# Unit scale of a scan-and-route kernel: from sums of squares ahead of the scan, in place of a largest value after it

## The chip, the cores and the metric

The kernel runs on one core of a Trainium2 chip. Its engines run side by side and meet through semaphores: TensorE (PE, with its weight loads as PEld), VectorE (DVE), ScalarE (ACT), GpSimd (POOL) and the DMA queues, of which SyncE (SP) issues most. The metric is the device time of one execution in microseconds (us).

## The reference

A gated recurrence feeds a mixture of experts in which each token goes to one expert.

```python
sig = 1.0 / (1.0 + np.exp(-f_logit))
f = lower_bound + (1.0 - lower_bound) * sig
i = 1.0 - f
for t in range(S):                       # S = 5056, batch 4, D = 256
    h = f[:, t] * h + i[:, t] * x[:, t]  # h starts at 0 for each sequence
    y[:, t] = h
...
logits = x @ w_gate                      # x: y as 20224 rows of 256
expert_idx = np.argmax(logits, axis=1)   # 8 experts
gate_w = softmax(logits)[expert_idx]
out[mask] = gate_w * (np.maximum(xe @ w1[e], 0.0) @ w2[e])   # F = 1024
```

## The kernel before

The 20224 tokens are cut into 79 units of 256. A unit lies with the 256 values of d on the partitions (two halves `c`) and its tokens along the free axis. Per unit `u`:

- `ahead` issues on SP's queue the loads of the gate input `ft` (`gate_load`, L264) and of `xt` (`load`, L269), four units ahead.
- `tanh` (L274) and two `affine` (L278) on ScalarE make the gate f in `ft`. `weigh` (L283, VectorE) turns `xt` into (f - 1) x, in place.
- `scan` (L305, VectorE) runs the recurrence in place in `xt`, one instruction for each half; it starts from the last column of the unit before. After it, L308 takes the largest absolute value of the unit for each partition, `am`.
- `split` takes that to all partitions: `all_max` (L115) multiplies `am`, broadcast to 128 columns, by half an identity, so that each row of a PSUM tile `tp` holds all 128 values; L319 and L320 on VectorE reduce it to the unit's scale, a power of two, in `m`. ScalarE writes the scaled high half of the unit as float16 (L323). `lower` (L330, VectorE) writes the low half, and SP issues a transposing DMA for each 128 tokens (L332).
- `logits` (L339) multiplies by the gate in eight short matmuls; `route` and `place` find each token's expert and its row in the bucket of that expert, and POOL scatters the rows (L399). Their many small VectorE instructions are handed out one at a time by `drip`, which is called at fixed places.

The expert stage gathers rows back from the buckets by transposing DMAs (`fetch`, L531, SP; three buffers `xT`), and does `gemm1` (L562 to L564, relu on ScalarE L567, the low half of it on VectorE L547) and `gemm2` (L598 to L600, ScalarE L604, POOL scatter L605). Every product is done as three float16 matmuls.

At the start the weights (16 loads of 1 MB) are scaled and split in two float16 halves: L178 and L182 on TensorE, L202 on ScalarE, L211 on VectorE. The second weights are loaded into the places of split first ones, so that those loads wait for L211. In this stage a scheduler orders the instructions. From then on the program order is the written one: a `step` does gemm1 of one pair of tiles and gemm2 of an earlier one, and calls `fill` at eight places of it, the slots. `plan_unit` gives the parts of a unit to slots: the split of unit u at slot 0, its `lower` and the tanh of unit u+2 at 1, loads of u+4 and the scan of u+1 at 2, the affines and `weigh` of u+2 at 2 and 3, the logits of u at 5. The next unit follows 5 to 8 slots later, the sooner the fewer rows are ready.

Of the kernel before, what the change touches and what calls it, by code (L numbers as in the profile page):

```python
# [17 lines left out]
P = 128  # L18
# [24 lines left out]
EXPM = 0x7F800000  # L43
EVEN = 0x7F000000
MAGIC = 12582912.0
INLINE = mybir.DependencyInfo(mybir.DependencyClass.NoSync, mybir.DependencyReason.SCHED_ONLY)
PACED = mybir.DependencyInfo(mybir.DependencyClass.Sync, mybir.DependencyReason.DATA)

# [17 lines left out]
def moe_kernel(ctx: ExitStack, tc: tile.TileContext, x, fl, lb, wg, w1, w2, cst, tok, out, xb, S):  # L66
# [43 lines left out]
    half = const.tile([P, P], BF16, tag="half", name="half")  # L110
    nc.vector.tensor_scalar_mul(half, ident, 0.5)

    def all_max(col, ps, rhs):

# [161 lines left out]
    def affine(u, c):  # L276
        ft = loaded[u][0]
        nc.scalar.activation(ft[:, c, :], ft[:, c, :], AF.Identity, scale=fs[:, c:c + 1], bias=fa[:, c:c + 1])  # L278

    def weigh(u):  # L280

        ft, xt = loaded[u]
        nc.vector.scalar_tensor_tensor(xt, ft, 1.0, xt, op0=ALU.subtract, op1=ALU.mult)  # L283

    def prep(u):

        tanh(u)
        affine(u, 0)
        affine(u, 1)
        weigh(u)  # L290

    def scan(u):

        ft, xt = loaded[u]
        t0 = u * UNIT
        cuts = [0] + [a for a in range(1, UNIT) if (t0 + a) % S == 0] + [UNIT]
        for c in range(2):
            for a, b in zip(cuts, cuts[1:]):
                if (t0 + a) % S == 0:
                    ini = 0.0  # L300
                elif a:
                    ini = xt[:, c, a - 1:a]
                else:
                    ini = loaded[u - 1][1][:, c, UNIT - 1:UNIT]
                nc.vector.tensor_tensor_scan(xt[:, c, a:b], ft[:, c, a:b], xt[:, c, a:b], ini, op0=ALU.mult, op1=ALU.subtract)  # L305
            drip(DRIP)
        am = sm.tile([P, 1], F32, tag="am", name=f"am{u}", bufs=4)
        nc.vector.tensor_reduce(am, xt, axis=AX.XY, op=ALU.max, apply_absolute_value=True)  # L308
        drip(DRIP)
        most[u] = am  # L310

    def split(u, rows, m, i0):

        ft, y = loaded[u]
        a = i0 // 2
        pt = ptp.tile([P, 512], F32, tag="tp", name=f"tp{u}")
# [7 lines left out]
        return pt, s, hl  # L324

    def lower(u, rows, pt, s, hl, i0):
# [6 lines left out]
        return hl, pt  # L333

    def logits(u, hl, pt, lg, i0):

        for i in range(2):
            for h in range(4):
                nc.tensor.matmul(pt[:, i * 3 * E:(i + 1) * 3 * E], lhsT=hl[:, i, h, :], rhs=gate[:, h % 2].rearrange("p k e -> p (k e)"), start=h == 0, stop=h == 3)  # L339
        nc.vector.tensor_reduce(lg[:, i0:i0 + 2, :], pt[:, 0:6 * E].rearrange("p (i k e) -> p i e k", i=2, k=3), axis=AX.X, op=ALU.add)  # L340

    def route(g, ng, lgt, m):
# [10 lines left out]
        mi = m.bitcast(I32)[:, 0, :nu]  # L353
        v.tensor_single_scalar(mi, mi, EVEN, op=ALU.bitwise_and)
# [62 lines left out]
    def tile_info(g, cnt, k, size):  # L417
# [29 lines left out]
        mk = sm.tile([P, 8, E], F32, tag="mk", name=f"mk{g}", bufs=4)  # L447
# [174 lines left out]
    NREST = N - taken  # L622
    NTAIL = (NREST + E * (P - 1)) // P

    loaded, gated, most, halves, owed = {}, [], {}, {}, []

    def gates(u):
        while len(gated) <= u and len(gated) < NU:
# [53 lines left out]
    def tick(u):  # L682

        def one():
            ahead(u + 4)
            if u + 1 < NU:
                scan(u + 1)

        def two(part):
            if u + 2 < NU:  # L690
                part(u + 2)
        first, second = (lambda: two(tanh)), (lambda: two(lambda v: affine(v, 0)))

        def third():
            two(lambda v: affine(v, 1))
            two(weigh)

        def three():
            g, a = where[u]
            gu = plan[g][0]  # L700
            if a == 0:
                grp[0] = (wk.tile([P, G, PITCH], F32, tag="rows", name=f"rows{g}", bufs=3),
                          sm.tile([P, 2, GRU], F32, tag="m", name=f"m{g}"),
                          sm.tile([P, G, E], F32, tag="lg", name=f"lg{g}"))
# [15 lines left out]
        return one, first, second, third, three, low, four  # L720

    queue, fetched, pend, nst = [], [], [], 0

# [45 lines left out]
    def scans(u):  # L769
        while scanned[0] <= u and scanned[0] < NU:  # L770
            preps(scanned[0])
            scan(scanned[0])
            scanned[0] += 1

    jobs = {}
    for p in range(E):
# [9 lines left out]
    for w in ORDER.split():  # L786
# [9 lines left out]
        elif k == "T":  # L796
            scans(u)
            t1 = tick(u)
            for part in t1[4:]:
                part()  # L800
            u += 1
        elif k == "A":
# [16 lines left out]
            step(lambda k: None, False)  # L819
    scans(u)  # L820
    preps(u + 1)
    ahead(u + 2)

    nc.vector.reciprocal(ui, wsc)
# [8 lines left out]
    def plan_unit(t1, period):  # L833

        nonlocal nxt
        scans1, tanh2, one2, other2, split1, lower1, logits1 = t1
# [135 lines left out]
```

## Time and profile before

| | |
|---|---|
| median of 3 runs | 1029.66 us (1029.53 to 1034.99) |
| profiled execution, its own time | 1019.52 us |
| its span, first to last instruction | 1017.6 us |
| TensorE busy | 931.3 us, 92% of the span |
| VectorE, ScalarE, GpSimd busy | 656.9, 499.4, 330.2 us |
| mean granted TensorE clock | 0.987 |

Busy times are sums over the span. Matmuls are pipelined, so each has a duration longer than its spacing: the spacing of starts says what one costs in a full queue.

### The profile page before, as it was taken

Reading aid. Unit: us, or ns where it says so; the run is one execution under the profiler, and the core shown is the slowest. Engines: PE = TensorE matmul, PEld = TensorE weight load, DVE = VectorE, ACT = ScalarE, POOL = GpSimd, SP = SyncE. Lnnn points to the kernel's source line nnn. Section 1 sums busy time; section 2 is a strip of 40 time slices with the busy share of each in tenths; the row PEclk is TensorE's granted clock in tenths of the full one; section 3 lists DMA queues with packets and bytes.
Section 4 is the critical chain, followed back from the end, with each engine's and each line's share of the span. In section 5 each row is a group of like instructions: output and inputs, shape, how many; then the busy total and the mean of one; then the engine's idle time right before and its main releaser. Section 6 shows DMA issues by size and latency. Waiting matters only on the chain.

```text
span 1017.6 us, 29588 instructions
## 1 busy us (share of the span) xinstructions
PE 931.3 (92%) x10971; PEld 850.5 (84%) x10971; DVE 656.9 (65%) x1816; ACT 499.4 (49%) x971; POOL 330.2 (32%) x326
## 2 busy tenths in 40 slices
PE   3538879999997999999999999999999999999994
PEld 2426779999986999998988999888888888899994
DVE  7898879887866787777878777676644322223220
ACT  4566545555555555555565555564433333333331
POOL 0151143433433334444443443334333111121111
PEclk9998999999999999999999999999999999999997
DMA  7997678778786887899998677775423222221210
GB/s 256 340 340 194 131 158 169 156 157 162 158 159 154 162 175 151 169 178 191 193 200 172 157 174 153 149 167 126 103 77 78 49 53 53 51 51 41 48 45 19
DMA packets 239774, 145.54 MB, mean 143 GB/s; under 512 B 205966, under 2 KB 207248, under 8 KB 237585
## 3 DMA queue, kind: packets, MB, share of 16 engines
q1 hardware_dynamic: 224272, 102.02, 47.5%
q0 software_dynamic: 15360, 41.60, 14.4%
q8 instruction: 94, 1.54, 0.7%
q14 instruction: 48, 0.39, 0.1%
HBM read 58.57 MB, written 43.16 MB: 100 GB/s over the span
## 4 chain that ended last, share of the span: by engine, by line
PE 72%; DVE 10%; DMA 8%; issue 3%; ACT 3%; SPq 2%; POOL 1%; POOLq 0%; ACTq 0%; DVEq 0%
PE g L562 12%; PE g L564 12%; PE g L563 12%; PE g L598 11%; PE g L599 11%; PE g L600 11%; DMA w2s<-in_w 3%; DMA ft<-in_f 3%; DVE xt L305 2%; DMA xT<-buckets 2%; DVE hT L547 2%; DVE ft L330 1%; PE wps L178 1%; PE tp L339 1%; SPq L531 1%
## 5 line engine op out<-in xcount | busy, mean ns | idle before, releaser
L562 PE MATMUL g<-xT,w1s 128*128 128x128 f16 (+1 forms) x1968 | 401.7, 237 | 11.5 <-DMA xT<-buckets 5.5
L564 PE MATMUL g<-xT,w1s 128*128 128x128 f16 (+1 forms) x1968 | 401.8, 237 | 0.0
L563 PE MATMUL g<-xT,w1s 128*128 128x128 f16 (+1 forms) x1968 | 401.8, 237 | 0.0
L598 PE MATMUL g<-w2s,hT 128*128 x1296 | 353.5, 273 | 3.8 <-DVE am L308 2.1
L600 PE MATMUL g<-w2s,hT 128*128 x1296 | 353.5, 273 | 0.0
L599 PE MATMUL g<-w2s,hT 128*128 x1296 | 353.4, 273 | 0.0
L547 DVE SCALAR_TENSOR_TENSOR hT<-g,hT 128x512 f16<-128x512 f32 x324 | 220.4, 686 | 205.0 <-ACT hT L567 202.8
L567 ACT ACTIVATE hT<-g 128x512 f16<-128x512 f32 x324 | 190.8, 593 | 128.9 <-PE g L564 123.3
L605 POOL DMA_INDIRECT out_dram<-ob,me x142 | 143.7, 1012 | 333.9 <-ACT ob L604 258.4
L399 POOL DMA_INDIRECT buckets<-rows,idx x158 | 166.3, 1053 | 259.6 <-ACT hT L567 162.5
L563 PEld LDWEIGHTS <-w1s 128*128 x1968 | 193.5, 98 | 17.5 <-issue 10.4
L562 PEld LDWEIGHTS <-w1s 128*128 x1968 | 193.4, 98 | 10.3 <-DMA xT<-buckets 1.5
L564 PEld LDWEIGHTS <-w1s 128*128 x1968 | 193.5, 98 | 7.1
L604 ACT ACTIVATE ob<-g,fac 128x256 f32<-128x256 f32 x162 | 76.3, 471 | 197.3 <-PE g L600 189.4
L599 PEld LDWEIGHTS <-hT 128*128 128x128 f16 x1296 | 126.8, 98 | 16.6 <-issue 2.9
L598 PEld LDWEIGHTS <-hT 128*128 128x128 f16 x1296 | 126.8, 98 | 16.4 <-issue 2.5
L600 PEld LDWEIGHTS <-hT 128*128 128x128 f16 x1296 | 126.8, 98 | 14.9
L305 DVE TENSOR_TENSOR_SCAN xt<-ft,xt,xt 128x256 f32<-128x256 f32 (+2 forms) x156 | 110.7, 728 | 0.0
L278 ACT ACTIVATE ft<-ft,fa,fs 128x256 f32<-128x256 f32 x158 | 91.1, 591 | 0.8
L330 DVE SCALAR_TENSOR_TENSOR ft<-xt,m,ft 128x256 f16<-128x256 f32 x158 | 72.6, 480 | 28.9 <-ACT ft L323 24.5
L323 ACT ACTIVATE ft<-xt,m 128x512 f16<-128x512 f32 x79 | 57.0, 721 | 69.5 <-DVE m L320 67.8
L274 ACT ACTIVATE ft<-ft 128x512 f32<-128x512 f32 x79 | 49.2, 622 | 64.7 <-DMA ft<-in_f 54.5
(128 smaller groups left out, 609.9 us busy)
## 6 DMA issues: line engine op xcount, KB each, us to landing
ft<-in_f SPq DMA_DIRECT2D x79, 256.0 KB
xt<-in_x SPq DMA_DIRECT2D x79, 256.0 KB
w2s<-in_w SPq DMA_DIRECT2D x14, 1024.0 KB
rows<-ft SPq DMA_TRANSPOSE x158
buckets<-rows,idx POOLq DMA_INDIRECT x158
out_dram<-ob,me POOLq DMA_INDIRECT x142
ws<-in_w SPq DMA_DIRECT2D x2, 1024.0 KB
xT<-buckets SPq DMA_TRANSPOSE x126
```

The lines of the kernel that those rows point to most:

```text
L278: nc.scalar.activation(ft[:, c, :], ft[:, c, :], AF.Identity, scale=fs[:, c:c + 1], bias=fa[:, c:c + 1])
L305: nc.vector.tensor_tensor_scan(xt[:, c, a:b], ft[:, c, a:b], xt[:, c, a:b], ini, op0=ALU.mult, op1=ALU.subtract)
L399: d = nc.gpsimd.indirect_dma_start(out=xb[:, :], out_offset=bass.IndirectOffsetOnAxis(ap=idx[:, i:i + 1], axis=0), in_=rows[:, i, 0:ROW], ...
L547: nc.vector.scalar_tensor_tensor(lo, ps, 0.0, hh, op0=ALU.max, op1=ALU.subtract)
L562: nc.tensor.matmul(o, lhsT=hi, rhs=xT[:, c, a:a + nt], start=c == 0, stop=False)
L563: nc.tensor.matmul(o, lhsT=hi, rhs=xT[:, 2 + c, a:a + nt], start=False, stop=False)
L564: nc.tensor.matmul(o, lhsT=lo, rhs=xT[:, c, a:a + nt], start=False, stop=c == 1)
L567: pace[:] = [nc.scalar.activation(hh, ps[:, :, :n], AF.Relu).ins.name]
L598: nc.tensor.matmul(po[:, :D], lhsT=hh, rhs=hi, start=f == 0, stop=False)
L599: nc.tensor.matmul(po[:, :D], lhsT=hh, rhs=lo, start=False, stop=False)
L600: nc.tensor.matmul(po[:, :D], lhsT=hl, rhs=hi, start=False, stop=f == NF - 1)
L605: d = nc.gpsimd.indirect_dma_start(out=out[:, :], out_offset=bass.IndirectOffsetOnAxis(ap=ti[j], axis=0), in_=ob, in_offset=None, bounds_c ...
```

## The change

The unit's scale no longer comes from the largest value of its result. `square` has ScalarE sum the squares of the raw `xt` for each partition (`am`), ahead of `tanh` in slot 1. `bound` has TensorE add, over all partitions, this sum and the squares of the last column of the unit before: three matmuls of one column, at slot 4 of unit u-2. `unit_scale` makes a power of two below one over the root from the bits of the sum, with two VectorE instructions at slot 6. What is gone: the reduction L308 with the `drip` behind it, `all_max` for units, L319 and L320. The gate's logits get a PSUM tile of their own. The scale is another number, and `route` undoes it accordingly.

```diff
+    def square(u):
+        am = sm.tile([P, 1], F32, tag="am", name=f"am{u}", bufs=4)
+        nc.scalar.activation(junk, loaded[u][1], AF.Square, accum_out=am)
+        most[u] = am
+    def bound(u):
...
+        pt = ptp.tile([P, 512], F32, tag="tp", name=f"mx{u}")
+        cols = [(upper16(most.pop(u)), oneb)]
+        if u * UNIT % S:
+            cols += [(h, h) for h in (upper16(loaded[u - 1][1][:, c, UNIT - 1:UNIT]) for c in range(2))]
+        for k, (a, b) in enumerate(cols):
+            nc.tensor.matmul(pt[:, 0:1], lhsT=a.to_broadcast([P, P]), rhs=b, start=k == 0, stop=k == len(cols) - 1)
+        most[u] = pt
+    def unit_scale(u):
...
+        nc.vector.tensor_scalar(m[:, 0, a:a + 1], most.pop(u).bitcast(I32)[:, 0:1], -0.5, ROOT, op0=ALU.mult, op1=ALU.add)
+        nc.vector.tensor_single_scalar(m[:, 1, a:a + 1], m[:, 0, a:a + 1], EXPM, op=ALU.bitwise_and)
     def prep(u):
+        square(u)
         tanh(u)
...
-        am = sm.tile([P, 1], F32, tag="am", name=f"am{u}", bufs=4)
-        nc.vector.tensor_reduce(am, xt, axis=AX.XY, op=ALU.max, apply_absolute_value=True)
-        drip(DRIP)
-        most[u] = am
...
-        all_max(most.pop(u), pt[:, P:2 * P], half)
-        nc.vector.tensor_reduce(m[:, 0, a:a + 1], pt[:, P:2 * P], axis=AX.X, op=ALU.max)
-        nc.vector.tensor_scalar(m.bitcast(I32)[:, 1, a:a + 1], m.bitcast(I32)[:, 0, a:a + 1], EVEN, EVEN, op0=ALU.bitwise_and, op1=ALU.bitwise_xor)
...
+        def first():
+            two(square)
+            two(tanh)
...
+        def spread():
+            two(bound)
+        def scaled():
+            two(unit_scale)
...
-        coming.extend((nxt + k, a) for k, a in ((0, split1), (1, lower1), (1, tanh2), (2, scans1), (2, one2), (3, other2), (5, logits1), (10, finish)))
+        coming.extend((nxt + k, a) for k, a in ((0, split1), (1, lower1), (1, tanh2), (2, scans1), (2, one2), (3, other2), (4, spread2), (6, scale2), (5, logits1), (10, finish)))
```

On TensorE, in a step of the middle of the run (`g` is the PSUM tile of the expert stage, `tp` that of `all_max`), there stands before:

```order
12542 L600 MATMUL g_36_0_10980<-w2s,hT_10671 128x256
12543 L115 LDWEIGHTS am_10897
12544 L115 MATMUL tp_10993<-half,am_10897 128x128
12545 L598 LDWEIGHTS hT_10671
12546 L598 MATMUL g_36_0_10980<-w2s,hT_10671 128x256
```

Now, in a step near it (`mx` is the tile of `bound`, `am` the sums of one unit, `xt` the result of the unit before it):

```order
12218 L588 MATMUL g_35_1_10685<-xT_10138,w1s 128x256
12219 L299 LDWEIGHTS am_10638
12220 L299 MATMUL mx_10700<-oneb,am_10638 128x1
12221 L299 LDWEIGHTS xt_10199
12222 L299 MATMUL mx_10700<-xt_10199 128x1
12223 L299 LDWEIGHTS xt_10199
12224 L299 MATMUL mx_10700<-xt_10199 128x1
12225 L586 ISA
```

One pair of weight load and matmul has become three, and what they read now includes a scan result (`xt`) that is two slots old in the written order.

On VectorE, one unit from its scale (`m`) to the scan of the next and the `weigh` of the one after it, before:

```order
1158 L319 TENSOR_REDUCE m_10662<-tp_10664 128x1
1159 L320 TENSOR_SCALAR m_10662<-m_10662 128x1
1160 L330 SCALAR_TENSOR_TENSOR ft_10091<-xt_10093,m_10662,ft_10091 128x256 x2
1161 L547 SCALAR_TENSOR_TENSOR hT_10671<-g_36_0_10672,hT_10671 128x512
1162 L305 SCALAR_TENSOR_TENSOR xt_10238<-ft_10236,xt_10093,xt_10238 128x256 x2
1163 L308 TENSOR_REDUCE am_10712<-xt_10238 128x1
1164 L547 SCALAR_TENSOR_TENSOR hT_10671<-g_36_1_10691,hT_10671 128x512
1165 L283 SCALAR_TENSOR_TENSOR xt_10419<-ft_10417,xt_10419 128x512
```

And now (the scale made here is that of a later unit than the one whose low half follows):

```order
1100 L308 TENSOR_SCALAR m_10617<-mx_10700 128x1
1101 L309 TENSOR_SCALAR m_10617<-m_10617 128x1
1102 L571 SCALAR_TENSOR_TENSOR hT_10667<-g_35_3_10742,hT_10667 128x512
1103 L353 SCALAR_TENSOR_TENSOR ft_10197<-xt_10199,m_10617,ft_10197 128x256 x2
1104 L337 SCALAR_TENSOR_TENSOR xt_10348<-ft_10346,xt_10199,xt_10348 128x256 x2
1105 L314 SCALAR_TENSOR_TENSOR xt_10509<-ft_10507,xt_10509 128x512
```

The long reduction between the scan and `weigh` is gone, and the scale no longer stands directly ahead of the low half that uses it.

On ScalarE, from a unit's high half (L323, now L346) to the gate of a later one, before:

```order
585 L567 ACTIVATE hT_12081<-g_43_3_12142 128x512
586 L323 ACTIVATE ft_11536<-xt_11538,m_11983 128x2x256
587 L274 ACTIVATE ft_11841<-ft_11841 128x512
588 L604 ACTIVATE ob_0_12212<-g_42_0_12178,fac_12079 128x256
589 L278 ACTIVATE ft_11841<-ft_11841,fa,fs 128x256 x2
```

And now:

```order
657 L591 ACTIVATE hT_12279<-g_43_3_12349 128x512
658 L346 ACTIVATE ft_11712<-xt_11714,m_11993 128x2x256
659 L286 ACTIVATE junk,am_12400<-xt_12045 128x512
660 L277 ACTIVATE ft_12043<-ft_12043 128x512
661 L628 ACTIVATE ob_0_12415<-g_42_0_12381,fac_12277 128x256
662 L281 ACTIVATE ft_12043<-ft_12043,fa,fs 128x256 x2
```

The squares of a unit stand right ahead of its tanh. Counted in matmuls of the expert stage, the units also stand up to 96 of 9792 earlier than before in the middle of the run (the logits of unit 30 after 2256 of them, before after 2352), because with one `drip` less for each unit the planner counts fewer ready rows and spaces units closer; up to unit 15 and from unit 62 on they stand where they stood.

## Rows read from the trace of the kernel before

**Rows 1.** Windows by stage: engines' busy us with counts, clock, DMA share, GB/s.

```profile
0.00:96.35 96.35, 45.67 (x384) 35.76 (x385) 81.70 (x217) 54.18 (x63) 18.16 (x18) 0.96 0.94 292
96.35:150.00 53.65, 43.92 (x632) 41.54 (x633) 42.92 (x134) 29.45 (x57) 16.96 (x16) 0.97 0.64 139
150.00:350.00 200.00, 189.90 (x2659) 176.94 (x2658) 161.60 (x502) 109.33 (x234) 75.72 (x75) 0.98 0.79 161
500.00:760.00 260.00, 260.00 (x2603) 233.81 (x2602) 184.08 (x504) 138.52 (x269) 105.39 (x106) 1.00 0.67 150
```

**Rows 2.** TensorE's waits from 96.35 to 1004 us: total us, times, longest.

```profile
PE tp L115 <- DVE am L308: 4.0, 4, 2.3
PE g L598 <- DVE am L308: 2.1, 1, 2.1
PE tp L339 <- ACT ft L323: 1.8, 1, 1.8
```

**Rows 3.** TensorE's timeline in full queues: start, us, instruction.

```profile
630.63 0.22 PE L115 MATMUL tp<-half,am 128*128 128x128 bf16 x1
630.69 0.27 PE L562 MATMUL g<-xT,w1s 128*128 128x256 f16 x1
...
637.37 0.27 PE L600 MATMUL g<-w2s,hT 128*128 x1
637.48 0.35 PE L339 MATMUL tp<-gate,ft 128*128 128x24 f16 x8
637.68 0.27 PE L562 MATMUL g<-xT,w1s 128*128 128x256 f16 x1
```

**Rows 4.** Groups by form, whole run: count, busy us, mean ns, idle before.

```profile
L115 PEld LDWEIGHTS <-am 128*128 128x128 bf16 x79 | 7.8, 99 | 17.8 <-DVE am L308 16.9
L319 DVE TENSOR_REDUCE m<-tp 128x1 f32<-128x128 f32 x79 | 22.5, 285 | 33.3 <-PE tp L115 28.7 <-issue 4.1
L320 DVE TENSOR_SCALAR m<-m 128x1 int32<-128x1 int32 x79 | 12.0, 152 | 2.4
L185 DVE TENSOR_SCALAR wm<-wps 128x2 f32<-128x2 f32 x8 | 1.2, 155 | 1.1 <-PE wps L182 1.1
L274 ACT ACTIVATE ft<-ft 128x512 f32<-128x512 f32 x79 | 49.2, 622 | 64.7 <-DMA ft<-in_f 54.5 <-issue 10.2
```

**Rows 5.** Windows of the start, columns as in rows 1.

```profile
12.00:16.00 4.00, 3.12 (x35) 2.68 (x33) 3.35 (x10) 0.91 (x2) 0.00 (x0) 1.00 0.37 142
16.00:20.00 4.00, 1.79 (x18) 1.44 (x16) 3.00 (x10) 3.25 (x5) 0.00 (x0) 1.00 0.57 135
```

**Rows 6.** The chain of waits in the start: start us, us, what.

```profile
59.06 2.36 DVE w1s L211
...
63.04 13.35 DMA w2s<-in_w
76.44 5.32 PE wps L178 x48
```

**Rows 7.** VectorE in 32 to 76 us: the window, then one group by form.

```profile
32.00:76.00 44.00, 17.75 (x162) 14.58 (x162) 42.23 (x114) 25.38 (x30) 17.47 (x12) 1.00 1.10 336
...
L308 DVE TENSOR_REDUCE am<-xt 128x1 f32<-128x512 f32 x6 | 4.1, 682 | 0.0
```

**Rows 8.** Timeline of VectorE and ScalarE in unit 68, in a full stretch.

```profile
630.89 0.29 DVE L319 TENSOR_REDUCE m<-tp 128x1 f32<-128x128 f32 x1
631.41 0.72 ACT L323 ACTIVATE ft<-xt,m 128x512 f16<-128x512 f32 x1
634.34 0.74 DVE L305 TENSOR_TENSOR_SCAN xt<-ft,xt,xt 128x256 f32<-128x256 f32 x1
```

**Rows 9.** ScalarE's waits from 150 to 500 us, columns as in rows 2.

```profile
ACT ft L274 <- DMA ft<-in_f: 39.5, 15, 7.8
```

**Rows 10.** Timeline around the logits of unit 34 and the scan of unit 35.

```profile
326.83 0.21 PE L339 MATMUL tp<-gate,ft 128*128 128x24 f16 x2 [1.82 <-ACT ft L323]
328.99 0.74 DVE L305 TENSOR_TENSOR_SCAN xt<-ft,xt,xt 128x256 f32<-128x256 f32 x1
```

More of the change, by code (lines that the diff above doesn't have):

```diff
@@ L45 @@
 MAGIC = 12582912.0
+ROOT = 197.25 * 2.0 ** 23
+TURN = float(EVEN)
 INLINE = mybir.DependencyInfo(mybir.DependencyClass.NoSync, mybir.DependencyReason.SCHED_ONLY)
@@ L109, in moe_kernel @@
     tri = const.tile([P, P], F16, tag="tri", name="tri")
-    half = const.tile([P, P], BF16, tag="half", name="half")
-    nc.vector.tensor_scalar_mul(half, ident, 0.5)
+    oneb = const.tile([P, 1], BF16, tag="oneb", name="oneb")
+    nc.vector.memset(oneb, 1.0)
+    junk = const.tile([P, 2, UNIT], BF16, tag="junk", name="junk")
     def all_max(col, ps, rhs):
@@ L278, in affine, with upper16 @@
         nc.scalar.activation(ft[:, c, :], ft[:, c, :], AF.Identity, scale=fs[:, c:c + 1], bias=fa[:, c:c + 1])
+    def square(u):
[3 more added lines that the diff above has]
+    def bound(u):
+        def upper16(t):
+            return t.bitcast(BF16)[:, 1:2]
+        pt = ptp.tile([P, 512], F32, tag="tp", name=f"mx{u}")
[6 more added lines that the diff above has]
+    def unit_scale(u):
+        g, a = where[u]
+        if a == 0:
+            scale_of[g] = sm.tile([P, 2, GRU], F32, tag="m", name=f"m{g}", bufs=4)
+        m = scale_of[g].bitcast(I32)
+        nc.vector.tensor_scalar(m[:, 0, a:a + 1], most.pop(u).bitcast(I32)[:, 0:1], -0.5, ROOT, op0=ALU.mult, op1=ALU.add)
+        nc.vector.tensor_single_scalar(m[:, 1, a:a + 1], m[:, 0, a:a + 1], EXPM, op=ALU.bitwise_and)
     def weigh(u):
@@ L315, in split @@
         a = i0 // 2
-        pt = ptp.tile([P, 512], F32, tag="tp", name=f"tp{u}")
-        all_max(most.pop(u), pt[:, P:2 * P], half)
-        nc.vector.tensor_reduce(m[:, 0, a:a + 1], pt[:, P:2 * P], axis=AX.X, op=ALU.max)
-        nc.vector.tensor_scalar(m.bitcast(I32)[:, 1, a:a + 1], m.bitcast(I32)[:, 0, a:a + 1], EVEN, EVEN, op0=ALU.bitwise_and, op1=ALU.bitwise_xor)
         s = m[:, 1, a:a + 1]
@@ L323, in split, with lower @@
         nc.scalar.activation(hl[:, :, 0:2, :], y.rearrange("p c (i t) -> p i c t", i=2), AF.Copy, scale=s)
-        return pt, s, hl
-    def lower(u, rows, pt, s, hl, i0):
+        return s, hl
+    def lower(u, rows, s, hl, i0):
         y, r16 = loaded[u][1], rows.bitcast(F16)
@@ L332, in lower, with logits @@
             nc.sync.dma_start_transpose(r16[:, i0 + i, 0:2 * D].rearrange("p (h d) -> p h d", d=P), hl[:, i].rearrange("p h t -> p (h t)"))
-        return hl, pt
-    def logits(u, hl, pt, lg, i0):
+        return (hl,)
+    def logits(u, hl, lg, i0):
+        pt = ptp.tile([P, 512], F32, tag="tp", name=f"tp{u}")
         for i in range(2):
@@ L352, in route @@
         nu = ng // 2
-        mi = m.bitcast(I32)[:, 0, :nu]
-        v.tensor_single_scalar(mi, mi, EVEN, op=ALU.bitwise_and)
+        mi = m.bitcast(I32)
+        v.tensor_scalar(mi[:, 0, :nu], mi[:, 1, :nu], -1.0, TURN, op0=ALU.mult, op1=ALU.add)
         l2, s2 = (t[:, :ng, :].rearrange("p (u i) e -> p u (i e)", i=2) for t in (lgt, sh))
@@ L446, in tile_info @@
         v.tensor_tensor(start, val[:, 0, :], pin[:, 1:], op=ALU.add)
-        mk = sm.tile([P, 8, E], F32, tag="mk", name=f"mk{g}", bufs=4)
+        mk = sm.tile([P, 8, E], F32, tag="mk", name=f"mk{g}", bufs=3)
         v.tensor_tensor(mk[:, :k], gt[:, :k, 1:], gt[:, :k, 0:E], op=ALU.subtract)
@@ L623, in moe_kernel @@
     NTAIL = (NREST + E * (P - 1)) // P
-    loaded, gated, most, halves, owed = {}, [], {}, {}, []
+    loaded, gated, most, scale_of, halves, owed = {}, [], {}, {}, {}, []
     def gates(u):
@@ L691, in two, with second @@
                 part(u + 2)
-        first, second = (lambda: two(tanh)), (lambda: two(lambda v: affine(v, 0)))
+        def first():
+            two(square)
+            two(tanh)
+        def second():
+            two(lambda v: affine(v, 0))
         def third():
@@ L702, in three @@
                 grp[0] = (wk.tile([P, G, PITCH], F32, tag="rows", name=f"rows{g}", bufs=3),
-                          sm.tile([P, 2, GRU], F32, tag="m", name=f"m{g}"),
+                          scale_of[g],
                           sm.tile([P, G, E], F32, tag="lg", name=f"lg{g}"))
@@ L719, in four @@
                 placing.append((g, 2 * (u - a), 2 * gu, rows, m, r))
-        return one, first, second, third, three, low, four
+        return one, first, second, third, spread, scaled, three, low, four
     queue, fetched, pend, nst = [], [], [], 0
@@ L771, in scans, with bounds @@
             preps(scanned[0])
+            bounds(scanned[0])
             scan(scanned[0])
             scanned[0] += 1
+    def bounds(u):
+        bound(u)
+        unit_scale(u)
     jobs = {}
@@ L798, in moe_kernel @@
             t1 = tick(u)
-            for part in t1[4:]:
+            for part in t1[6:]:
                 part()
@@ L821, in moe_kernel @@
     preps(u + 1)
+    bounds(u + 1)
     ahead(u + 2)
@@ L835, in plan_unit @@
         nonlocal nxt
-        scans1, tanh2, one2, other2, split1, lower1, logits1 = t1
-        coming.extend((nxt + k, a) for k, a in ((0, split1), (1, lower1), (1, tanh2), (2, scans1), (2, one2), (3, other2), (5, logits1), (10, finish)))
+        scans1, tanh2, one2, other2, spread2, scale2, split1, lower1, logits1 = t1
+        coming.extend((nxt + k, a) for k, a in ((0, split1), (1, lower1), (1, tanh2), (2, scans1), (2, one2), (3, other2), (4, spread2), (6, scale2), (5, logits1), (10, finish)))
         coming.sort(key=lambda c: c[0])
```

## The prediction

> **What bounds the kernel now.** I read the busy times by stage first, then TensorE's waits, then the start. The stages [rows 1] show three regimes. Up to 96.35 us, where the first expert matmul starts, TensorE is busy less than half of the time, VectorE 81.70 of 96.35 us, and the DMA engines are near full. From 96.35 to 350 us TensorE has gaps: 53.65 - 43.92 = 9.7 us and 200 - 189.90 = 10.1 us. From 500 to 760 us it has none, and the last units end there. So in the late stage nothing that VectorE or ScalarE does is worth anything; there only the number and spacing of TensorE's own instructions count. The change can win in the start and in the gaps of the middle.
>
> Of the gaps, the ones with the old scale in them are listed as waits for `am` [rows 2]: 4.0 us in four waits of the `all_max` matmul itself and 2.1 us in one that stood just behind such a matmul, together 6.1 us. The 1.8 us of the logits behind the high half has another origin, below.
>
> **TensorE's own instructions.** In a full queue the old `all_max` takes the spacing to the next start, 630.69 - 630.63 = 0.06 us; the eight short logits matmuls, each with its own weight load, take 637.68 - 637.48 = 0.20 us, 25 ns each [rows 3]. The three one-column matmuls are like those: 3 x 25 = 75 ns, against about 56 ns. For the 68 units whose scale falls into the expert stage (11 to 78) that is 68 x 0.019 = 1.3 us more. The bounds: nothing, if three accumulating columns cost what one matmul did, and 68 x 2 x 0.099 = 13 us, if each of the two added pairs held the queue for the whole of its weight load, whose row gives 99 ns [rows 4]. I take 1.3 us, since the logits rows are the same kind of pair.
> The Trainium skill has a rule against the change here: in "TensorE: Matmul & The Clock Gate", section "LDWEIGHTS (loading the stationary operand)", a weight load takes its columns divided by 1.2 ns, 107 ns for 128 columns however little is multiplied. If that were the spacing, my estimate from that page is 68 x 2 x 0.107 = 15 us more. The rows of the logits disagree, as loads run ahead there.
>
> **VectorE.** Per unit go L308 at 0.68 us [rows 7], L319 at 0.285 and L320 at 0.152 [rows 4]. Two small instructions come; the trace has the like in L185, one that reads PSUM, 0.155 us, and L320, 0.152 us. Net 0.81 us less per unit, 64 us over 79. In the late stages this is idle time for idle time. In the start it counts: from 32 to 76 us VectorE is busy 42.23 of 44 us, and six of the reductions fall there [rows 7], 6 x 0.81 = 4.9 us. The chain [rows 6] shows why that is on the path: L211 ends at 61.42 us, only then are the next weights loaded into the place it read, 13.35 us, and the weight norms (L178) start when they have landed. But those loads share engines that are full: the DMA share is 1.10 over 32 to 76 us [rows 7]. Time can be won only where they had room, 4 x 0.63 + 4 x 0.43 = 4.2 us between 12 and 20 us [rows 5]. There SP's queue stands behind the transposes of unit 0, which wait for its scale; they now come sooner, since the scale is ready before the scan ends. So the start gains between 0 (another order by the scheduler, with ScalarE's squares ahead of its weight splits) and 4.2 us. I take 3 us.
>
> **ScalarE.** It gets 79 squares of 128x512, priced like its tanh at 0.622 us [rows 4], 49 us in all. In the expert stage it is busy 109.33 of 200 us [rows 1]; with 0.62 us more per unit of some 8 us its share goes from 55 to about 63%. What hides it is that idle time; a relu that comes 0.6 us later is covered by four PSUM buffers, that is four slots of 1.3 us. If that cover were gone, each unit would cost TensorE up to 0.62 us, 42 us over 68 units; no row points there. The square waits for `xt`, and stands ahead of tanh, so that ScalarE now waits for both loads; in the middle SP issues `xt` ahead of `ft`, so `ft` stays the later.
>
> **The new wait.** `bound` of unit u+2 stands in TensorE's queue two slots behind the scan of u+1, where it reads the last column; before, the first thing on TensorE to need that scan was `all_max` at slot 0 of the next unit, 5 to 8 slots on. Behind `bound` on TensorE stands the whole expert stage, and everybody waits for that. How much room is there? In a full stretch, unit 68: the scan ends at 634.34 + 0.74 = 635.08 us [rows 8]. `bound` stands 12 wide matmuls ahead of the logits, which started at 637.48; at 0.11 us each [rows 3] TensorE passes that place at 636.2. It has 1.1 us to spare. Nothing is freed there by the lost `all_max`, for the high half at 631.41 came behind a relu, not behind L319 at 630.89. In the late middle this room is gone: the logits of unit 34 would have started at 326.83 - 1.82 = 325.0 us, the place of `bound` was 1.3 us earlier, 323.7, and the scan ended at 328.99 + 0.74 = 329.73 [rows 10], 6 us late. What is late there is the gate load: ScalarE waits 39.5 us in 15 waits for `ft` between 150 and 500 us, the longest 7.8 [rows 9], and that also gave the 1.8 us of rows 2. Those loads stand in SP's queue behind gathers, which wait for a free `xT`, and the change does nothing for them; by the written orders the units come up to 96 expert matmuls earlier, some 5 us, but so do their loads. A stall is not paid again by the next unit, since all that is behind TensorE catches up with it. The bounds for the new wait: nothing, if the 0.81 us per unit and the direct start of the high half restore the room, and 15 late loads x 1.1 us of lost room = 16 us, if each shows in full. I take 4 us, nearer to the low end, for TensorE's comparable waits in this trace, 4.0 + 2.1 + 1.8 us, were of that size with this lateness.
>
> **The sum.** Start -3.0; waits for `am` -6.1; new wait +4.0; short matmuls +1.3: -3.8 us. Against the profiled execution's own 1019.52 us (its span of 1017.6 and 1.9 around it) that is 1015.7. The median of the runs shown is 1029.66, 10 us above that execution, which I can't attribute to a place in the program; the difference is taken from it, so 1025.9 us, rounded to 1026.
>
> **The rivals.** About 0.5% of the time, 5.1 us, is what can be told from no change.
> 1. More is won: the start gives its full 4.2 us, the waits for `am` go, the new one costs nothing, and the first expert steps (9.7 us of gaps before 150 us, where VectorE is busy 42.92 of 53.65 us [rows 1]) lose half of what is left beside the 2.1 us, 3.8 us. -4.2 - 6.1 - 3.8 + 1.3 = -12.8: 1017 us. For it: VectorE is loaded at 80% there. Against: the rows wait on transfers as well. Chance 0.22.
> 2. The change does not do what it says for TensorE: the waits for `am` turn into waits at `bound` of the same length, the start is set by the loads. 1.3 us slower, 1031, no change. For it: the cause, late gate loads, is untouched. Chance 0.20.
> 3. Slower: `bound` becomes the place where TensorE waits for VectorE. It decides once the scan of a unit ends later than two slots (some 2.7 us) behind its place, as in unit 34; at 16 us for 15 such units, less 6.1, plus 1.3, the time is 11 us more with nothing won in the start: 1041. Against: in full stretches 1.1 us is left. Chance 0.13.
> 4. Each short pair holds the queue for its weight load: +13 - 6.1 - 3 + 4 = +8 us, 1038. The logits rows speak against it. Chance 0.04.
> The forecast, 1020 to 1031, has the remaining 0.41.
>
> **How the numbers follow.** Faster by over 0.5% means below 1024.5: rival 1 and nearly half of the forecast, 0.22 + 0.18 = 0.40. Slower, above 1034.8: rivals 3 and 4 and a little of rival 2, 0.19. The rest, 0.41, is within 0.5%. The range reaches to a little beyond rival 1 and into rivals 3 and 4: 1015 to 1036. The forecast's own range is 1020 to 1031.
>
> **What would show it.** The first expert matmul starts at 93 us or so, not at 96.35: the start is right. VectorE's busy sum falls to about 593 us and ScalarE's rises to about 548. No gap of TensorE is put down to `am` of a reduction; waits of the `mx` matmuls for L337 (the scan) between 150 and 350 us add up to about 4 us. The three matmuls take 75 ns up to the next start in a full stretch. The prediction is wrong if those `mx` waits are above 10 us in all, if the start doesn't move or gets longer, or if from 500 to 760 us TensorE has gaps at all.

## The result, and the profile after

The changed kernel took 1036.19 us, the median of 20 runs, against 1029.67 us for the kernel before, run beside it: a ratio of 1.006, with a 95% interval of 1.0042 to 1.0079. In another group of runs, at the end, it was 1.0035 (1.0018 to 1.0052). That is a small loss where 1026 us was forecast. The profiled execution took 1036.02 us, with a span of 1034.3.

The windows by stage of the kernel after answer to [rows 1]:

```profile
0.00:95.10 95.10, 41.95 (x407) 34.07 (x408) 75.78 (x212) 60.11 (x84) 14.85 (x18) 0.84 0.95 296
95.10:150.00 54.90, 44.34 (x592) 40.56 (x593) 37.85 (x122) 31.33 (x65) 16.13 (x14) 0.94 0.57 135
150.00:350.00 200.00, 186.06 (x2620) 170.78 (x2617) 141.31 (x477) 120.87 (x275) 73.33 (x72) 0.99 0.77 155
500.00:760.00 260.00, 259.62 (x2641) 233.28 (x2640) 166.85 (x485) 149.48 (x321) 103.38 (x104) 1.00 0.67 152
```

From 150 to 350 us VectorE is busy 20.3 us less than in rows 1 (141.31, not 161.60), ScalarE 11.5 us more, and TensorE, which was to gain from it, 3.8 us less. TensorE's waits in the expert stage, from its first matmul at 95.1 us, answer to [rows 2] (the largest; what waited, for what; us in total, times, longest):

```profile
PE g L586 <- issue: 5.0, 13, 0.5
PE tp L363 <- issue: 4.4, 7, 1.2
PE g L587 <- issue: 3.8, 9, 0.5
PE g L586 <- DVE hT L571: 3.7, 3, 1.9
PE g L588 <- issue: 3.2, 6, 1.1
PE g L622 <- issue: 2.6, 12, 0.4
PE g L586 <- DMA xT<-buckets: 2.5, 2, 2.3
PE mx L299 <- DVE xt L337: 1.5, 3, 0.6
```

The waits for `am` are gone and the new ones at `bound` (L299) are small, as forecast. But most of the list now says "issue": TensorE stood, and nothing that the profile shows held it. The timeline of TensorE shows what such a stall is like (start, us, instruction, idle before):

```profile
154.18 0.22 PE L586 MATMUL g<-xT,w1s 128*128 128x128 f16 x1
154.91 0.23 PE L587 MATMUL g<-xT,w1s 128*128 128x128 f16 x1 [0.51 <-issue]
154.97 0.22 PE L588 MATMUL g<-xT,w1s 128*128 128x128 f16 x1
155.65 0.22 PE L586 MATMUL g<-xT,w1s 128*128 128x128 f16 x1 [0.45 <-issue]
156.36 0.23 PE L587 MATMUL g<-xT,w1s 128*128 128x128 f16 x1 [0.50 <-issue]
```

These matmuls sit in the middle of an accumulation, with weights and data that were there long before. In a full queue they start 56 ns apart; here single ones come every 0.7 us. One that comes alone counts its whole 0.22 us as busy, so the idle time is only a part of what a stall costs. And right behind this stall the clock falls. Windows on both sides of 158 us (TensorE is first behind the comma; the last three numbers are the granted clock, the DMA share and GB/s):

```profile
155.00:158.00 3.00, 1.20 (x12) 0.58 (x11) 0.00 (x0) 0.12 (x1) 1.31 (x2) 1.00 1.06 151
158.00:161.00 3.00, 3.00 (x26) 2.31 (x24) 2.28 (x11) 1.84 (x5) 0.00 (x0) 0.50 0.93 190
```

After 3 us with 12 matmuls in them TensorE goes on at the lower of its two levels, 1.2 GHz (granted 0.50). The first profile of the kernel before had hardly any of this, while its median was 10 us above that profile. So the first question for the chip was whether the change makes these stalls, or the first profile was no example of the runs that were timed.

### The profile page after: what moved, and what is told of

The parts are those of the page before. It is cut to its first block, busy times and chain, and to the rows that moved or that the text cites. A ratio compares the mean times of both kernels' runs of the same rounds, so it can differ in the third digit from the quotient of the medians.

```text
span 1034.3 us, 29980 instructions
## 1 busy us (share of the span) xinstructions
PE 937.2 (91%) x11127; PEld 851.5 (82%) x11127; DVE 595.7 (58%) x1737; ACT 540.4 (52%) x1129; POOL 325.6 (31%) x326
## 3 DMA queue, kind: packets, MB, share of 16 engines
q8 instruction: 95, 1.56, 0.7%
## 4 chain that ended last, share of the span: by engine, by line
PE 80%; DVE 6%; issue 4%; DMA 3%; ACT 3%; SPq 2%; another core or an unknown queue 1%; POOL 0%; POOLq 0%; DVEq 0%; ACTq 0%
PE g L622 13%; PE g L586 13%; PE g L587 13%; PE g L588 13%; PE g L623 13%; PE g L624 13%; PE tp L363 1%; DMA ft<-in_f 1%; DMA w2s<-in_w 1%; DVE w1s L214 1%; DVE xt L337 1%; PE wps L181 1%; ACT w2s L205 1%; DVE hT L571 1%
## 5 line engine op out<-in xcount | busy, mean ns | idle before, releaser
L586 PE MATMUL g<-xT,w1s 128*128 128x128 f16 (+1 forms) x1968 | 402.9, 237 | 11.5 <-issue 5.0
L423 POOL DMA_INDIRECT buckets<-rows,idx x158 | 161.6, 1023 | 279.3 <-ACT hT L591 163.5
L281 ACT ACTIVATE ft<-ft,fa,fs 128x256 f32<-128x256 f32 x158 | 91.8, 592 | 1.0
L314 DVE SCALAR_TENSOR_TENSOR xt<-ft,xt 128x512 f32<-128x512 f32 x79 | 54.4, 689 | 52.5 <-ACT ft L281 35.4
L277 ACT ACTIVATE ft<-ft 128x512 f32<-128x512 f32 x79 | 48.9, 621 | 27.3 <-DMA ft<-in_f 24.4
```

The lines of the kernel that those rows point to most:

```text
L423: d = nc.gpsimd.indirect_dma_start(out=xb[:, :], out_offset=bass.IndirectOffsetOnAxis(ap=idx[:, i:i + 1], axis=0), in_=rows[:, i, 0:ROW], ...
L586: nc.tensor.matmul(o, lhsT=hi, rhs=xT[:, c, a:a + nt], start=c == 0, stop=False)
```

## The experiments

In the table a gap is 300 us less TensorE's busy time in the window from 200 to 500 us of the profile; "issue" is what the list of waits puts down to issue there, which I call the stalls. "Places" says where the written order puts the middle units on TensorE: as in the kernel before, as in the change (36 to 96 expert matmuls earlier), or later than either. Ratios are to the kernel before on the same chip, whose own median stands in the last column.

| kernel | places | ratio (95%) | gap, us | issue, us | before there, us |
|---|---|---|---|---|---|
| before, first profile | before | | 11.07 | 1.5 | |
| before_again | before | 0.9992 (0.9969 to 1.0015) | 6.81 | 5.3 | 1028.68 |
| two_more | before | 0.997 (0.9947 to 0.9994) | 7.03 | 6.3 | 1028.68 |
| sq_before | before | 1.001 (0.999 to 1.003) | 9.86 | 7.3 | 1028.70 |
| drip_back | before | 0.9984 (0.9962 to 1.0007) | 9.68 | 7.8 | 1028.70 |
| slots_before | before | 0.999 (0.9965 to 1.0015) | 10.47 | 6.8 | 1030.39 |
| the change | change | 1.006 (1.0042 to 1.0079) | 14.94 | 11.9 | 1029.67 |
| after_again, one run, 1029.74 us | change | | 11.92 | 7.3 | 1028.68 |
| after_third | change | 1.0035 (1.0018 to 1.0052) | 13.97 | 10.0 | 1028.49 |
| less_drip | change | 1.008 (1.0052 to 1.0108) | 14.29 | 11.8 | 1028.70 |
| slots_after | change | 1.0049 (1.003 to 1.0069) | 13.70 | 11.4 | 1030.39 |
| no_carry | change | 1.006 (1.0033 to 1.0087) | 15.79 | 10.7 | 1028.68 |
| late_bound | change | 1.0067 (1.0044 to 1.009) | 15.80 | 10.1 | 1028.70 |
| min6 | later | 1.0024 (1.0001 to 1.0047) | 14.78 | 10.6 | 1030.39 |
| plus1 | later | 1.0296 (1.0255 to 1.0336) | 14.99 | 13.5 | 1030.39 |
| plain_after2 | change | 0.9963 (0.9948 to 0.9977) | 7.08 | 6.0 | 1028.49 |
| plain_after | change | 0.9894 (0.9856 to 0.9931) | 2.10 | 1.8 | 1015.12 |
| plain_before | before | 0.9858 (0.9823 to 0.9894) | 0.56 | 0.2 | 1015.12 |
| drip_back2 | before | 1.0022 (0.9994 to 1.0051) | 10.02 | 2.8 | 1015.12 |
| back_late | before | 0.9998 (0.9975 to 1.0021) | 11.43 | 1.0 | 1015.12 |

**Both kernels again, unchanged.**

> The kernel before, unchanged, for a second profile of it. Theory A (TensorE's instructions arrive late, in either kernel, and the first profile of before was of a quiet execution): the stalls of TensorE that the waits put down to issue in the expert stage, 3.4 us in the first profile of before and 31.2 us in the one of after, are 10 us or more here, and the profiled execution is near 1029. Theory B (the change itself makes these stalls): they stay below 6 us here, and the 10 us between the first profile and the median lie in waits for transfers. Time either way 1030, the same.

> The changed kernel, unchanged, for a second profile. Theory A: stalls put down to issue vary from one execution to the next, here anything from 10 to 35 us, and the time follows them; those for am, the scan and hT stay as they were, some 8 us together. Theory B: 25 to 35 us of issue again.

TensorE's waits in the expert stage of before_again:

```profile
PE g L562 <- DVE hT L547: 6.7, 3, 4.7
PE g L562 <- issue: 4.1, 6, 1.3
PE g L563 <- issue: 3.3, 7, 0.8
PE g L564 <- issue: 3.3, 9, 0.6
PE g L562 <- DMA xT<-buckets: 1.7, 2, 1.1
```

Theory A holds: the kernel before has the stalls too. With four smaller ones its rows with "issue" sum to 14.0 us; those of the first profile sum to 1.5. And no wait for `am` is left in the list, where [rows 2] had 6.1 us. The same holds in two_more, sq_before, less_drip and slots_after, the other kernels with the old scale that show these stalls: 0 to 0.4 us. Where the stalls stand, that gain is not to be had. The idle time of the two profiles of the kernel before is nearly the same, 86.3 and 87.5 us; the later one, whose span is 8.4 us longer, has 7.2 us more of busy time for the same 10971 matmuls. Two things that go with the stalls lie in that busy time: matmuls that come alone, and a lower clock where the stalls are thickest. These are the windows of before_again:

```profile
94.00:150.00 56.00, 46.03 (x578) 41.45 (x578) 39.11 (x117) 26.83 (x51) 14.57 (x13) 0.88 0.53 125
150.00:200.00 50.00, 43.20 (x565) 38.97 (x564) 35.56 (x125) 23.22 (x50) 15.94 (x16) 0.90 0.57 139
```

In the first profile the clock is 0.98 and 0.99 there, and 662 and 712 matmuls are run. Where that profile ran is not known; with 1019.52 us and hardly a stall it is like the chip of 1015.12 us further down. In after_again the rows with "issue" sum to 14.5 us, in the first profile of the change to 20.8: single profiles differ by some 6 us.

**The new matmuls and the square, each by itself.** no_carry turns the condition in `bound` into `if False:`, two_more adds to `split` of the kernel before

```diff
+        for k in range(2):
+            all_max(am, pt[:, 256 + k:257 + k], half[:, 0:1])
```

and sq_before adds `square`, as in the change, to the kernel before.

> The changed kernel with one short matmul for a unit's scale in place of three: the squares of the carried state are left out of it. The place of the instruction and all else stays. Theory A or B by the number of TensorE's instructions: 156 pairs fewer and no wait for the scan; 1036 falls by the wait (2.6 us) and 156 pairs at 25 ns (3.9 us, of which 68 units lie in the expert stage) to about 1031. Theory C (the cost is on ScalarE and in the order of the work, not in these matmuls): 1035 to 1036.

> The kernel before with two further one-column matmuls per unit, ahead of the old one, that go to a column nobody reads: the number of TensorE's instructions is that of the change, without its other parts. Spacing of 25 ns each: 68 x 2 x 0.025 = 3.4 us slower at most, 1031 to 1033. If more instructions also bring more stalls put down to issue: 1035 or more. If each pair held the queue for its weight load of 99 ns: 13 us, 1043.

> The kernel before with ScalarE's square of each unit's raw input added ahead of its tanh; its sum is read by nobody. Theory R: ScalarE is busy 49 us more, and TensorE does not notice: 1027 to 1030. Theory S: 1032 to 1036, with more waits of TensorE for hT and of the high half.

Neither costs anything that can be measured. two_more, with 158 more short pairs, came out 0.3% faster, for which I have no cause. sq_before says that ScalarE's 79 squares are hidden. And no_carry, without the wait for the scan and with a third of the short matmuls, is as slow as the change.

**The matmuls later.** late_bound calls `bound` and `unit_scale` for unit u+1 at slots 3 and 4 of unit u.

```diff
-(4, spread2), (6, scale2),
+(3, spread2), (4, scale2),
```

> The changed kernel with the three short matmuls and the two small instructions on VectorE a whole unit later (for unit u+1 at slots 3 and 4 of unit u, instead of u+2 at 4 and 6), so that the scan and the square that they read ended a unit earlier. The waits of these matmuls for the scan and the squares (3.6 and 7.3 us in the two profiles of the change) go to below 1 us. If that is the loss: 1029 to 1032. Theory R: what is won there comes back as other stalls, 1033 to 1036. A scale that is ready only one slot ahead of its use may hold ScalarE's high half, up to 3 us more.

No wait of L299 for a scan or a square is left in its list of waits (one of 2.6 us for another instruction of ScalarE is), and the ratio is 1.0067: the new wait is not the loss either.

**The step of the routing generator.** The change drops, with the reduction, the call of `drip` behind it. drip_back puts one back behind the change's scan, less_drip takes it out of the kernel before and does nothing else:

```diff
         nc.vector.tensor_reduce(am, xt, axis=AX.XY, op=ALU.max, apply_absolute_value=True)
-        drip(DRIP)
```

> The changed kernel with one more step of the routing generator behind each scan, as before: by the written order the units in the middle (24 to 66) then stand again where they stood before, instead of 36 to 96 expert matmuls earlier. Theory R (the changed rhythm makes TensorE's stalls between 200 and 500 us: 23.2 and 19.7 us in the two profiles of the change, 11.9 in the second one of before): some 12 to 14 us of stalls there and a time of 1028 to 1031. Theory S (ScalarE's squares and the new wait for them): 1034 to 1036, stalls as in the change.

> The kernel before with the one step of the routing generator behind the reduction left out: its units stand where those of the change stand, all else is as before. Theory R: 1033 to 1036 and 18 us or more of stalls between 200 and 500 us. Theory S: 1028 to 1030.

This is the whole loss: 0.9984 with the step and 1.008 without it, one in the changed kernel and one in the old. How one call reaches TensorE's order is seen in the planner's own numbers as each program is built (unit, then rows ready and first slot, before and in the change):

```
unit   before: ready slot   change: ready slot
  15           768    32             256    32
  16           768    38             256    37
  18           768    49             512    47
  33           512   136             768   132
  54           512   267             768   263
  66          2048   346            2048   346
```

With one step less, the tiles of a group are known to the planner one call later. At unit 15 it counts 256 rows in place of 768 and sets the next unit five slots on, not six; such steps add up to four slots by unit 33. The windows from 200 to 500 us of before_again, drip_back, less_drip and the change, in this order:

```profile
200.00:500.00 300.00, 293.19 (x4066) 272.96 (x4064) 238.78 (x687) 171.57 (x360) 119.96 (x119) 1.00 0.81 170
```

```profile
200.00:500.00 300.00, 290.32 (x4078) 270.17 (x4076) 207.72 (x631) 186.25 (x421) 117.51 (x117) 1.00 0.82 169
```

```profile
200.00:500.00 300.00, 285.71 (x3935) 263.06 (x3934) 230.41 (x662) 163.28 (x345) 117.40 (x115) 1.00 0.80 164
```

```profile
200.00:500.00 300.00, 285.06 (x4002) 263.71 (x4000) 202.15 (x619) 181.73 (x413) 117.85 (x116) 1.00 0.79 166
```

The first number behind the comma is TensorE's busy time: 293 and 290 us with the old places, 286 and 285 with the new. VectorE's (the third) and ScalarE's (the fourth) go with the kind of scale, and TensorE does not follow them.

**The places, or the steps?** The two lists replace the planner's rule and leave the steps as they are.

```diff
-            plan_unit(tick(u), 5 if r < LOW else 6 if r < MID else 7 if r < HIGH else 8)
+            nxt = SLOT[u - 9]
+            plan_unit(tick(u), 0)
```

> The changed kernel with the place of each unit in the expert stage written out as a list, that of the kernel before; the routing generator has its step less per unit, as in the change. Theory P (the places of the units make the loss): 1027 to 1031, and some 12 to 16 us of stalls between 200 and 500 us. Theory G (the later steps of the generator themselves, by the gathers and scatters that come later from them): 1033 to 1036 with 20 us or more of stalls there.

> The kernel before, the generator's step included, with the places of the units in the expert stage from a list, that of the change. Theory P: 1033 to 1036 and 20 us or more of stalls between 200 and 500 us. Theory G: 1027 to 1031.

It is the places: 0.999 for the changed kernel with the old ones, 1.0049 for the old kernel with the new ones.

**Later places.** In drip_back, `5 if r < LOW` is dropped (min6), or each period below 8 slots is one slot longer (plus1).

> drip_back with six slots, in place of five, from one unit to the next where few rows are ready: the middle units stand 70 to 240 expert matmuls later than in the kernel before. If fewer units per time are what TensorE's stalls follow, they fall below 14 us between 200 and 500 us and the time to 1020 to 1026. If the kernel before stood at its best, TensorE waits for gathered rows or in the planner's flush instead: 1030 or more.

> drip_back with one slot more between units at every level of ready rows (6, 7, 8 and 8 in place of 5, 6, 7 and 8). Theory P with no other bound: 1015 to 1024, stalls between 200 and 500 us at 10 us or less. With rows as the next bound: 1030 or more, in waits for xT.

Later is no better, 1.0024 and 1.0296: my reading that fewer units per time mean fewer stalls falls. The gap of min6 is as large as that of the change and its ratio lower (with intervals that overlap), so the gap of this one window is only a rough measure of the time. plus1 has gaps from 500 to 760 us as well, 260 - 248.55 = 11.5 us, where the others have 1.1 us at most.

**What the stalls are.** The plain kernels replace, after the start, the transposing transfer of the rows:

```diff
+            if early:
                 nc.sync.dma_start_transpose(...)
+            else:
+                nc.sync.dma_start(r16[:, i0 + i, 0:2 * D], hl[:, i].rearrange("p h t -> p (h t)"))
```

> The changed kernel with the transposing transfers of the rows, from the 11th unit on, replaced by plain copies of the same bytes between the same tiles: the order and the count of all instructions stay, and the rows of those units hold values in another order, so that the experts compute on other data. Theory D (the stalls of TensorE that no semaphore ends are instructions that arrive late, because the DMA engines are full of short packets): these stalls fall from 13 to 20 us between 200 and 500 us to below 6, and the time by 10 us or more, to 1025 or less. Theory N (they have nothing to do with the transfers): 1033 or more, stalls as before; what ScalarE waits for the gate's loads falls all the same.

> The kernel before with the same replacement. If Theory D holds and the places of the units matter only by these transfers, it is as fast as the changed kernel with them, within 3 us. If the places matter by themselves, some 7 us stay between the two.

> drip_back with the three short matmuls a unit later, as in late_bound: both the places of the kernel before and no wait for the scan or the square. The waits for the scan in drip_back's profile (2.7 us with the start) go; 1023 to 1027, a little below the kernel before. If a scale that is ready late holds ScalarE's high half: 1029 or more.

> drip_back once more, for a narrower interval: whether the change with the old places of the units is faster than the kernel before. First ratio 0.9984 (0.9962 to 1.0007); expected 0.997 to 1.000, not clear of no change.

These four shared a chip on which the kernel before takes 1015.12 us, not 1029, and TensorE has hardly any stalls of the kind shown above (1.5 us of "issue" in back_late, 3.4 in drip_back2). So the plain pair could not tell what the stalls are. It gains 1.1 and 1.4% there, where there are hardly any stalls to lose, and the intervals of the two ratios overlap, so that nothing follows on the places. What the chip did show is the changed kernel without its stalls, the case in which the prediction was argued, though with the old places; the change itself was not run there. TensorE's waits of drip_back2:

```profile
PE mx L299 <- DVE xt L337: 7.8, 12, 1.6
PE mx L299 <- ACT junk L286: 2.9, 1, 2.9
```

Here the new wait is real: 7.8 us at `bound` for the scan, against 6.1 us of old waits for `am` in [rows 2], and the ratio is 1.0022, no change. Of the gap of 10.02 us 2.8 are stalls, 6.9 are waits with a releaser. In back_late the wait moves on, to 5.7 us behind the scale's own instruction (L308), and the ratio is 0.9998. Both had been expected a little below 1.

> The changed kernel once more. So far two kinds of chip were met: those on which the kernel before takes 1029 us and TensorE has 9 us or more of stalls between 200 and 500 us that nothing in the profile ends, and one on which it takes 1015 and has next to none. On the first kind: a ratio of 1.005 to 1.008 again. On the second: if the places of the units cost only by those stalls, 0.998 to 1.003, with 8 us or more of waits for the scan; if they cost in another way too, 1.005 or more.

> The changed kernel with plain copies in place of the rows' transposes, once more. On a chip of the first kind this tells what the first time could not: Theory D (the stalls are instructions that come late behind the transfers): the stalls of TensorE that nothing ends fall below 6 us between 200 and 500 us, and the ratio is 0.98 or less. Theory N: they stay at 12 us or more, and the ratio is 0.99 or more. On a chip of the second kind: 0.989 again.

This chip has the stalls, and the ratio of the change is 1.0035, a smaller loss than the 1.005 to 1.008 expected. The windows of after_third and of plain_after2, the last three numbers being the clock, the DMA share and GB/s:

```profile
200.00:500.00 300.00, 286.03 (x4012) 264.91 (x4011) 203.75 (x625) 182.85 (x414) 118.96 (x116) 1.00 0.75 165
```

```profile
200.00:500.00 300.00, 292.92 (x4114) 273.07 (x4112) 209.96 (x644) 188.16 (x423) 122.15 (x118) 1.00 0.68 171
```

With the plain copies the DMA share falls from 0.75 to 0.68, TensorE's gap from 13.97 to 7.08 us and the ratio from 1.0035 to 0.9963, some 7 us. Theory D wanted 0.98 or less and Theory N 0.99 or more with the stalls unchanged; the result lies between them. Of the 7 us of gap some 4 are stalls (10.0 us down to 6.0), the rest are other waits. It is one profile each, where three of the change as it stands have 7.3 to 11.9 us; before 200 us the stalls stay, 8.1 and 7.7 us; and on the other chip the same copies gained 1.1% with hardly a stall to lose. So a part of the load of transfers in the stalls is hinted at, and not shown. The clock of this window is at its upper level of 2.4 GHz in both (granted 1.00), so it is not the clock that sets them apart.

## Why the prediction was wrong

**The step that failed** is in the part on the new wait: "by the written orders the units come up to 96 expert matmuls earlier, some 5 us, but so do their loads". I saw the shift and priced it at nothing. It is the only part of the change that measurably costs: less_drip alone gives 1.008, slots_after 1.0049, and the change with the old places 0.9984 and 0.999. On the chips with stalls the gaps are 6.81 to 10.47 us with the old places, 8.8 on average in the five kernels with a profile there, and 11.92 to 15.80 with the new, 14.3 in seven: 5.5 us more, beside 6.5 us between the medians. Of that 3.8 us are stalls, 6.7 us on average with the old places and 10.5 with the new. That the places cause the loss is shown, in both kernels and both ways, on chips with stalls; without them only the plain pair tried it, and could not tell. How they do it is not shown: the stalls have no releaser in the profile, fewer short packets take only part of the gap away, and later places make it larger too. With the old places the rest of the change gains 1.2 us by the medians of drip_back (1027.52 against 1028.70 us) and nothing by those of slots_before (1030.74 against 1030.39), neither clear of no change; the sum had 3.8.

**The base of the sum** was the second fault. The 10 us between the profile and the median, which I set aside as something that I "can't attribute to a place in the program", were stalls of TensorE, with the lone matmuls and the lower clock that go with them, as before_again shows. They stood in place of just those waits on which -6.1 us rested: 6.1 us in the first profile, none in before_again.

**The start, -3.0 us: mis-sized**, at its lower bound. First expert matmul at 96.35 and 94.03 us before, at 95.10, 94.06 and 94.40 after; in sq_before, with the squares and the old scale, at 94.41. The means of the first two sets are 0.7 us apart, less than the 2.3 us between the two profiles of one kernel, so the prediction's own sign for a right start (93 us) did not come. The clock is not the reason: its mean up to 94 us is 0.84, 0.98 and 0.66 in the three profiles of the change, which does not go with these times. TensorE's waits in the first 95 us of the change:

```profile
PE tp L363 <- ACT ft L346: 16.8, 5, 5.9
PE wps L181 <- DMA w2s<-in_w: 8.4, 4, 4.1
PE mx L299 <- ACT junk L286: 6.3, 3, 3.1
```

and of the kernel before, from its first profile:

```profile
PE wps L178 <- DMA w2s<-in_w: 12.2, 4, 7.5
PE tp L115 <- DVE am L308: 11.2, 7, 3.4
PE tp L339 <- ACT ft L323: 5.7, 2, 4.1
```

The mechanism was right: the 11.2 us for `am` are gone and the weights land earlier. In this profile it was given back on ScalarE, whose high halves now stand behind the squares and the gates. In the chain of waits of the change this is one stretch:

```profile
64.14 5.07 DMA w2s<-in_w
69.21 0.69 ACT junk L286 x2
69.90 1.04 ACT ft L277 x2
70.94 0.98 ACT ft L281 x2
71.92 0.61 ACT junk L286 x2
...
75.31 0.71 ACT ft L346
...
76.37 5.21 PE wps L181 x64
```

The load ends at 69.21 us, where that of [rows 6] ended at 76.39; the weight norms then start at 76.37 us, as before at 76.44. The squares themselves are 1.3 of the 6.1 us up to 75.31; the rest is the gate (L277, L281), a part of the weights and 1.1 us of "issue". I had priced ScalarE as hidden by the idle time of the expert stage, and had not asked the same of the start.

**The new wait, +4.0 us: right in place.** Its size depends on the chip: the waits of L299 for VectorE's results and the squares are 2.0, 5.8 and 3.3 us in three profiles of the change (1.5 + 0.5, 3.1 + 2.7, 2.1 + 0.9 + 0.3), and 10.7 us in drip_back2. As rival 3 it did not decide: late_bound has it no longer and is as slow. By the letter another of the prediction's signs of being wrong came: the change has 0.4 us of gaps from 500 to 760 us. They are put down to issue, and not to this wait.

**The short matmuls, +1.3 us: right.** In a full stretch of the change:

```profile
641.73 0.17 PE L299 MATMUL mx<-oneb,am 128*128 128x1 bf16 x1
641.76 0.19 PE L299 MATMUL mx<-xt 128*128 128x1 bf16 x2
641.81 0.27 PE L622 MATMUL g<-w2s,hT 128*128 x1
```

Three take 641.81 - 641.73 = 80 ns, forecast 75. Rival 4 falls; two_more says the same by its time. With it falls the estimate that I worked out from the Trainium skill ("TensorE: Matmul & The Clock Gate", section "LDWEIGHTS (loading the stationary operand)") as if each weight load set the spacing.

**VectorE and ScalarE.** VectorE's busy sum is 595.74 us (forecast 593). ScalarE's is 540.37 (548), though each square is two instructions. These are groups of the change by form, then ScalarE's timeline of one square:

```profile
L286 ACT ACTIVATE junk<-xt 128x512 bf16<-128x512 f32 x79 | 49.1, 621 | 9.3 <-DMA xt<-in_x 8.7 <-issue 0.5
L286 ACT ACTIVATION_READ_ACCUMULATOR junk<-xt 128x1 f32 x79 | 15.1, 191 | 0.0
L308 DVE TENSOR_SCALAR m<-mx 128x1 int32<-128x1 int32 x79 | 11.7, 148 | 2.1 <-PE mx L299 2.1
```

```profile
649.25 0.62 ACT L286 ACTIVATE junk<-xt 128x512 bf16<-128x512 f32 x1
649.77 0.19 ACT L286 ACTIVATION_READ_ACCUMULATOR junk<-xt 128x1 f32 x1
649.86 0.62 ACT L277 ACTIVATE ft<-ft 128x512 f32<-128x512 f32 x1
```

The square lasts what the tanh row promised, 0.62 us; the instruction of 0.19 us that reads its sum was not in my count. But these overlap: from the start of the square to the start of the tanh behind both it is 0.61 us, and the busy sum, in which an overlap counts once, rose by 41 us, not by the 49 of my count. The two small VectorE instructions, 148 and 152 ns, are within 7 ns of their stand-ins.

## What to carry to other kernels

When an edit drops a call that also paces something else, such as the `drip` here, compare the order that results and price that shift by itself; here it was all of the loss that was measured, and putting back one line undid it (0.9984; on the chip without stalls the kernel with that line has 1.0022, and the change without it was not run; no version that I ran with the rows' transposes is clearly faster than the kernel before, but for two_more's unexplained 0.997). Where the profiled execution is well below the median, find out what fills the difference before pricing waits that it shows, because what fills it may stand where they stood. And where work moves to an engine with idle time, ask whether it is idle in each stage on which the sum rests.

## What the runs showed of the hardware that was not expected

The same kernel takes 1015 us on one chip and 1028 to 1030 us on five groups of runs elsewhere. The difference shows in the profile as TensorE waiting for nothing: half a microsecond at a time, several times in a row, amid an accumulation, and before some 500 us (later 8.3 us in plus1 and at most 0.4 in the others). The clock is granted at 1.00 while they last in the timeline above, and falls to 0.50 behind them; from 200 to 500 us it is 0.99 or 1.00 in every profile. They look like instructions that arrive late. The profile page's list of queues of the change has one of kind "instruction":

```profile
q8 instruction: 95, 1.56, 0.7%
```

The Trainium skill ("Runtime: NRT & Kernel Launch", section "Instruction fetch mechanics") says that an engine's instructions come in 16 KiB blocks over a DMA queue of its own, and that this is mostly hidden. The block size agrees with this row, 1.56 MB in 95 packets. That it is hidden would agree with the one chip (1.5 us of "issue" in back_late) and not with the others, if these stalls are that; no run here shows that they are, and back_late, with hardly a stall, has the very same row.
